# The first block of a convolution and MLP kernel: shift convolution in PSUM, a plan that knows of one shared port, carried spectra made last

## The chip, the cores and the metric

The kernel runs on one core of a Trainium2 chip. TensorE (PE in the profile) multiplies matrices into PSUM; VectorE (DVE) and ScalarE (ACT) work element by element on SBUF and PSUM; GpSimd (POOL) works on SBUF only; SyncE (SP) issues all DMAs of this kernel in one queue, in program order. The metric is the device time of one execution in microseconds, the median of the runs shown. Lower is better.

## The reference

Two kinds of layer alternate, twice: x = x + A(layernorm(x)), then x = x + B(layernorm(x)). x is 2048 tokens by 1024 channels, all in float32.

```python
def _A_ref(q, k, v, shift_k, ssm_k, ssm_D):
    k_shift = jnp.zeros_like(k)
    for t in range(ks):                       # ks = 4, causal, per channel
        k_shift = k_shift + k_pad[:, t:t + S, :] * shift_k[:, ks - 1 - t][None, None, :]
    kv = k_shift * v
    ...                                       # y = causal convolution of kv with ssm_k over all S, by FFT
    y = y + kv * ssm_D[None, None, :]
    return q * y                              # q = layernorm(x)
def _B_ref(x, w1, b1, w2, b2):
    h = jnp.einsum("bsd,df->bsf", x, w1) + b1
    h = relu(h) ** 2
    return jnp.einsum("bsf,fd->bsd", h, w2) + b2
```

k, v and the filter are the same in both A layers, so the long convolution's result y is computed once. F, the hidden width of B, is 3584.

## The kernel before

The 2048 tokens are four blocks of 512 (T). The long convolution is a blocked one: a block of 512 tokens is two halves of 256 (BL), each half is turned into a spectrum by matmuls with cosine and sine tables, spectra of inputs and of filter pieces are multiplied and added up, and matmuls turn them back. The complex product is done with three real ones: each spectrum is kept in three kinds (real part, imaginary part, and a sum or difference), and PAIRS says which kind of x meets which kind of the filter. The filter's spectra of a later block need a part of the block before, the "carried" spectrum, kept in DRAM as KD.

After the first block the kernel is one long list of steps: matmuls of the MLP on TensorE, each float32 product as three matmuls of a rounded part and a remainder (lines 327 to 329), and beside them the convolution's further blocks, spread over the steps by a pace (fwd_x, fwd_g, prod_stream). What this change touches most is the part before: first_block.

first_block has to do, before the MLP can start, for each of eight channel blocks c of 128 channels: load k, v and the filter; the shift convolution (line 1102 on ScalarE for the first tap, line 1105 three times on VectorE for the others, all in SBUF) and its product with v (line 1108, GpSimd or VectorE); TensorE's transposes (412) and forward matmuls for x (1076) and for the filter; the three kinds of each spectrum (ScalarE's 1124 and 1163, VectorE's 1126, 1165, 1167); the carried spectrum (TensorE, ScalarE's copy 1178, a store); the products per token half jj (1246, 1251, 1253), their combination (1257, 1258) and a butterfly (669, 670); the inverse matmuls; the gated output (1277), a copy of y for the second A layer (1280, stored as YD) and the residual add (1285). All these matmuls go through the helper fmm, so that they share line 1076. The D term enters as an addition to the filter's first row: line 1143, a VectorE add on one partition. LayerNorm's statistics (1187 and the small steps 1193 to 1207) are taken for two token tiles at a time at the start, and again at the end on the new x ("tail"), whose normalised rows TensorE transposes (1314); they are split into a rounded part and a remainder (1321, 1323). Four hidden tiles' weights (eight halves) are split as well (1333, 1334), and their matmuls on the first 256 tokens are the first MLP matmuls (327 to 329, 256 wide).

The order of all this is made by a planner, the class Plan. Each piece is a task with one or more possible engines and a cost on each, with the tiles it reads and writes. Tiles stand in rings of a few buffers, and a ring's buffers are given out in the order in which they were asked for. order() simulates the list: of the tasks that are ready it takes the one that can start earliest, and among these the one with the lowest priority value; rank is added to that value, so that the carried spectrum's matmuls (rank 2e6) come when nothing else is ready. 400 tries with varied priorities are made when the kernel is built, and the best is issued, engine by engine, in that order. The costs are the formulas v_cost, v2_cost (VectorE with two SBUF operands), g_cost and a_cost; DMAs are one engine "D" with 2 us of latency. Before, each engine was free of the others.

fill() issues transposes that nobody reads, to keep TensorE going; FILL has their numbers at three places: in the last inverse matmuls of the first block (38), in a later stage (45), and in the tail (17).

The buffers that matter here: sx and sg, the spectra (four channel blocks each); the banks p1 (two), p2 (four) and pt (two) in PSUM; and room within xh and xl, which hold the MLP's input later and in the first block k, the filter and the products.

Of the kernel before, what the change touches and what calls it, by code (L numbers as in the profile page):

```python
# [41 lines left out]
PLAN_TRIES = 400  # L42
NORM_0 = "VA"
# [6 lines left out]
FILL = (38, 45, 17)  # L50
# [45 lines left out]
class Plan:  # L96
# [37 lines left out]
    def order(self, rise, noise):  # L134
# [12 lines left out]
        while ready:  # L147
            best = None
            for i in ready:
# [20 lines left out]
            _, i, (e, c, st) = best  # L170
            _, _, _, bufs, lat, _ = self.tasks[i]
            free[e] = st + c
            end[i] = st + c + lat
# [13 lines left out]
    def run(self):  # L187
# [3 lines left out]
        for i in reversed(range(n)):  # L191
            opts, _, deps, _, lat, _ = self.tasks[i]
            self.height[i] += min(c for _, c in opts) + lat
            for d in deps:
                self.height[d] = max(self.height[d], self.height[i])
                self.after[d].append(i)
        rng = np.random.default_rng(1)
        best = None
        for k in range(PLAN_TRIES):
# [6 lines left out]
            got = self.order(rise, noise.tolist())  # L206
            if best is None or got[0] < best[0]:
                best = (*got, rise, noise)
# [13 lines left out]
def v2_cost(n):  # L222
    return 250 + 1.3 * n


def g_cost(n):
    return 200 + 2.45 * n
# [7 lines left out]
def tile_h3_mlp(ctx: ExitStack, tc: tile.TileContext, q, kT, vT, shk, ssmT, ssmD, w1, b1, w2, b2,  # L235
# [54 lines left out]
    V.memset(epst, EPS)  # L290

# [129 lines left out]
    def fwd_g(sb, c):  # L421
# [38 lines left out]
        V.tensor_add(oa[0], oa[1], k0)  # L460
# [50 lines left out]
    def prod_stream():  # L511
# [152 lines left out]
    def flat(t, e):  # L664
        return t[:, e].rearrange("p (n c) -> p n c", c=CG)

# [376 lines left out]
    def first_block():  # L1043
# [8 lines left out]
        def sub(tag, n, off, shape, nm="xh"):  # L1052
# [3 lines left out]
            def make():  # L1056
                v = big[nm].t[:, off + i * size:off + i * size + size]
                return v if len(shape) == 2 else v.rearrange("p (a b) -> p a b", a=shape[1])
# [8 lines left out]
        with tc.tile_pool(name="pro", bufs=1) as pro:  # L1067
# [31 lines left out]

            def x_part(c, k4, v4):  # L1100
                ks = new(cv, "fx", 4, [P, T])
                pl.add([("A", a_cost(T))], lambda e: A.activation(
                    ks.t, k4.t[:, 3:], AF.Copy, scale=shkt[:, c, 0:1]), [k4], [ks])
                for q_ in range(1, 4):
                    pl.add([("V", v2_cost(T))], lambda e, q_=q_: V.scalar_tensor_tensor(
                        ks.t, k4.t[:, 3 - q_:T + 3 - q_], shkt[:, c, q_:q_ + 1], ks.t,
                        op0=OP.mult, op1=OP.add), [k4], [ks], lat=130)
                pl.add([("G", g_cost(T)), ("V", v2_cost(T))], lambda e: ENG[e].tensor_mul(
                    ks.t, ks.t, v4.t), [v4], [ks])
# [5 lines left out]
                for r in range(2):  # L1115
# [8 lines left out]
                    pl.add([("A", a_cost(T))], lambda e, r=r, oi=oi: A.copy(spread(sp[r].t), sums(oi.t)), [oi], [sp[r]])  # L1124
                    if r:
                        pl.add([("V", v_cost(T))], lambda e, oi=oi: V.tensor_add(
                            spread(sp[2].t), sums(oi.t), spread(sp[0].t)), [oi, sp[0]], [sp[2]])
                for i in range(3):
                    dma(lambda i=i: dview(XD[i], 0, c), lambda i=i: sp[i].t, [sp[i]])

            def g_load(c):
                raw = sub("lg", 2, 1560, [P, T])
                aux = sub("la", 2, 2584, [P, P])
# [3 lines left out]
                dma(lambda: aux.t[0:1], lambda: bass.AP(tensor=ssmD.tensor, offset=ssmD.offset + c * P,  # L1137
                                                   ap=[[0, 1], [1, P]]), w=[aux], cost=10)
                return raw, aux

            def g_part(c, raw, aux):
# [8 lines left out]
                for r in range(2):  # L1150
# [11 lines left out]
                    if r == 0:  # L1162
                        pl.add([("A", a_cost(T))], lambda e, o=o: A.copy(spread(sp[0].t), sums(o.t)), [o], [sp[0]])
                    else:
                        pl.add([("V", v_cost(T))], lambda e, o=o: V.tensor_add(
                            spread(sp[2].t), sums(o.t), spread(sp[0].t)), [o, sp[0]], [sp[2]])
                        pl.add([("V", v_cost(T))], lambda e, o=o: V.tensor_sub(
                            spread(sp[1].t), sums(o.t), spread(sp[0].t)), [o, sp[0]], [sp[1]])
                o = bank("p1", 2, ps1)
                kd = new(cv, "fk", 2, [P, T])  # L1170

                def mmk(e):
                    for r in range(2):
                        for h in range(2):
                            s_ = slice(h * BL + P, h * BL + BL)
                            fmm(o.t[:, (2 * r + h) * P:(2 * r + h + 1) * P], base.t[:, 2 * h + r], raw.t[:, s_], True, True)
                pl.add([("PE", 900)], mmk, [*keys, *tabs], [o], rank=2e6)
                pl.add([("A", a_cost(T))], lambda e: A.copy(kd.t, o.t), [o], [kd])
                dma(lambda: KD[0][c], lambda: kd.t.rearrange("p (r n) -> p r n", r=2), [kd])
                for i in range(3):  # L1180
                    dma(lambda i=i: dview(GD[i], 0, c), lambda i=i: sp[i].t, [sp[i]])
# [8 lines left out]
            def moments(st, n):  # L1190
# [7 lines left out]
                pl.add([("V", 80)], lambda e: V.tensor_scalar(ve.t, mv.t[:, :, 1], EPS, None, op0=OP.add),  # L1198
                       al, [ve], lat=130)
                pl.add([("A", 190)], lambda e: A.activation(sd.t, mv.t[:, :, 1], AF.Sqrt, bias=epst), al, [sd])  # L1200
                pl.add([("V", 80)], lambda e: V.reciprocal(r.t, sd.t), [sd], [r], lat=130)
                pl.add([("V", 130)], lambda e: V.tensor_mul(t.t, r.t, r.t), [r], [t], lat=130)
                pl.add([("V", 130)], lambda e: V.tensor_mul(t.t, t.t, ve.t), [ve], [t], lat=130)
# [676 lines left out]
```

## Time and profile before

| what | value |
|---|---|
| median of three runs | 2758.64 us (2758.22 to 2763.38) |
| the profiled execution | 2754.0 us |
| its span, first to last instruction | 2752.2 us |
| mean granted TensorE clock | 0.995 |
| VectorE busy | 2010.1 us |
| GpSimd busy | 922.5 us |

A page of the profile describes one execution. "Busy" of an engine is the time in which one of its instructions was running, with whatever that instruction waited for once issued; the idle time before an instruction is given with the instruction that released it. A row of the table by window has, for each engine, busy us and the number of instructions, then the granted clock, the share of the DMA engines' time and the data rate. The time of the first block is the stretch from 0 to about 140 us.

### The profile page before, as it was taken

The page shows a single profiled execution, that of the slowest core. Times are in us where ns is not written, and L with a number is a line of the kernel's source. Part 1 is how long each engine was busy: PE and PEld are TensorE (multiplying, and loading weights), DVE is VectorE, ACT ScalarE, POOL GpSimd, SP SyncE. Part 2 cuts the span into 40 slices and gives each one's busy share as a digit, 9 for nine tenths or more (in the row PEclk, how much of TensorE's full clock was granted, in tenths as well). Part 3 has the DMA queues.
Part 4 walks back from the last instruction along what each step waited for, and adds up shares of the span by engine and source line. Part 5 has one row for each costly group of instructions (what it writes and reads, how often), then busy time and mean ns, then how long its engine had stood idle before and what let it go on. Part 6 is the DMA issues. An engine that isn't in the chain of part 4 may idle for free.

```text
span 2752.2 us, 36801 instructions
## 1 busy us (share of the span) xinstructions
PE 2696.8 (98%) x12632; PEld 2238.5 (81%) x12632; DVE 2010.1 (73%) x3109; ACT 1121.7 (41%) x1935; POOL 922.5 (34%) x655
## 2 busy tenths in 40 slices
PE   7899999899999999999999999999999999999999
PEld 6888787788888888888888888888788788878887
DVE  8879888779888877788777665366687666664555
ACT  4254344343444333342234422254455444445443
POOL 6926665155542655326544454000100010001000
PEclk9999999999999999999999999999999999999999
DMA  8489988689989898788987877688888866676546
GB/s 261 164 295 334 306 294 288 238 281 376 345 290 316 306 335 298 257 318 294 344 280 250 314 277 266 226 290 304 297 289 294 281 228 210 230 258 208 176 165 203
DMA packets 378876, 755.86 MB, mean 275 GB/s; under 512 B 43704, under 2 KB 160576, under 8 KB 378688
## 3 DMA queue, kind: packets, MB, share of 16 engines
q1 hardware_dynamic: 378688, 753.50, 79.7%
q8 instruction: 100, 1.64, 0.2%
q14 instruction: 88, 0.72, 0.1%
HBM read 603.41 MB, written 149.95 MB: 274 GB/s over the span
## 4 chain that ended last, share of the span: by engine, by line
PE 84%; DVE 6%; DMA 5%; POOL 2%; issue 1%; ACT 1%; SPq 1%; DVEq 0%; ACTq 0%; POOLq 0%
PE p L327 26%; PE p L329 26%; PE p L328 26%; DMA whl<-wd_m 1%; DMA wr<-w 1%; PE pt L329 1%; PE pt L328 1%; PE pt L327 1%; DVE whl L1005 1%; DMA cg<-gd 1%; DMA whl<-wd_t 1%; PE p L1076 1%; PE pt L446 0%; PE pt L412 0%; PE pt L588 0%
## 5 line engine op out<-in xcount | busy, mean ns | idle before, releaser
L517 POOL TENSOR_TENSOR cp<-cx,cg 128x384 f32<-128x384 f32 (+5 forms) x288 | 540.9, 1891 | 587.7 <-DVE sm L521 383.6
L327 PE MATMUL p<-xh,whl 128*128 128x512 f32 (+1 forms) x1840 | 707.7, 385 | 2.0 <-DMA whl<-wd_m 1.9
L329 PE MATMUL p<-xh,whl 128*128 128x512 f32 (+1 forms) x1840 | 703.8, 382 | 0.6 <-POOL whl L1005 0.6
L328 PE MATMUL p<-xl,whl 128*128 128x512 f32 (+1 forms) x1840 | 703.6, 382 | 0.3 <-DVE xl L1323 0.3
L997 ACT CAST whl<-wr 128x512 fp32r<-128x512 f32 x638 | 384.4, 618 | 458.1 <-PE p L329 269.6
L1005 DVE TENSOR_TENSOR whl<-wr,whl 128x512 fp32r<-128x512 f32 x624 | 506.1, 831 | 72.9 <-ACT whl L997 66.9
L327 PE MATMUL p<-whl,rh 128*128 128x512 f32 x1372 | 547.4, 399 | 6.1 <-DMA whl<-wd_m 4.5
L328 PE MATMUL p<-whl,rh 128*128 128x512 f32 x1372 | 542.4, 395 | 4.2 <-DVE whl L1005 4.2
L329 PE MATMUL p<-whl,rl 128*128 128x512 f32 x1372 | 541.8, 395 | 0.0
L327 PEld LDWEIGHTS p<-xh,whl 128*128 128x128 f32 x1840 | 346.4, 188 | 71.0 <-DMA whl<-wd_m 2.0
L329 PEld LDWEIGHTS p<-xh,whl 128*128 128x128 f32 x1840 | 346.2, 188 | 68.9 <-POOL whl L1005 0.8
L328 PEld LDWEIGHTS p<-xl,whl 128*128 128x128 f32 x1840 | 346.2, 188 | 66.4 <-DVE xl L1323 0.5
L327 PEld LDWEIGHTS p<-whl,rh 128*128 128x128 f32 x1372 | 258.8, 189 | 67.3 <-DMA whl<-wd_m 7.7
L328 PEld LDWEIGHTS p<-whl,rh 128*128 128x128 f32 x1372 | 258.9, 189 | 63.7 <-DVE whl L1005 6.4
L329 PEld LDWEIGHTS p<-whl,rl 128*128 128x128 f32 x1372 | 258.7, 189 | 60.3
L1504 POOL TENSOR_TENSOR acc<-acc,px 128x512 f32<-128x512 f32 x18 | 23.1, 1323 | 774.7 <-DMA px<-b 774.7
L1407 DVE TENSOR_TENSOR rl<-wr,rh 128x512 fp32r<-128x512 f32 x140 | 142.2, 1016 | 179.9 <-ACT rh L1402 179.8
L521 DVE TENSOR_REDUCE sm<-cp 128x128 f32<-128x384 f32 (+5 forms) x288 | 249.0, 873 | 7.9 <-POOL cp L517 7.9
L1399 ACT ACTIVATE wr<-p,b1t 128x512 f32<-128x512 f32 x138 | 95.2, 690 | 371.6 <-PE p L329 369.8
L1468 DVE TENSOR_TENSOR rl<-wr,rh 128x256 fp32r<-128x256 f32 x84 | 49.4, 588 | 206.4 <-ACT rh L1463 206.3
L1527 DVE TENSOR_TENSOR acc<-p,acc 128x512 f32<-128x512 f32 x152 | 101.2, 687 | 89.2 <-PE p L329 88.6
L1460 ACT ACTIVATE wr<-p,b1t 128x512 f32<-128x512 f32 x84 | 57.9, 689 | 187.5 <-PE p L329 187.5
(270 smaller groups left out, 3437.1 us busy)
## 6 DMA issues: line engine op xcount, KB each, us to landing
whl<-wd_m SPq DMA_DIRECT2D x382, 512.0 KB, 5.6
wr<-w SPq DMA_DIRECT2D x494, 256.0 KB, 5.2
wr<-td SPq DMA_DIRECT2D x152, 256.0 KB, 4.4
wd_m<-whl SPq DMA_DIRECT2D x70, 512.0 KB, 6.5
cx<-xd SPq DMA_DIRECT2D x48, 512.0 KB, 5.4
cg<-gd SPq DMA_DIRECT2D x48, 512.0 KB, 6.9
gd<-fg SPq DMA_DIRECT2D x72, 256.0 KB, 6.2
cx<-xd SPq DMA_DIRECT2D x48, 384.0 KB, 6.0
```

The lines of the kernel that those rows point to most:

```text
L327: PE.matmul(o, lh, rh, start=start, stop=False)
L328: PE.matmul(o, lh, rl, start=False, stop=False)
L329: PE.matmul(o, ll, rh, start=False, stop=stop)
L517: G.tensor_mul(pr.rearrange("p c i -> p i c"), xt[:, 0:j + 1], gt[:, j::-1])
L521: V.tensor_reduce(sm[:, ty, jj], st["pr"], axis=AX.X, op=OP.add)
L997: A.copy(t[:, 0], raws[n]["t"])
L1005: ENG[e[n % len(e)]].tensor_sub(t[:, 1], raws[n]["t"], t[:, 0].bitcast(F32))
L1399: A.activation(r, st["o"], AF.Relu, bias=b1t[:, st["f"]:st["f"] + 1])
L1407: V.tensor_sub(st["lo"], st["r"]["t"], st["hi"].bitcast(F32))
L1460: A.activation(r, st["o"], AF.Relu, bias=b1t[:, st["f"]:st["f"] + 1])
L1468: V.tensor_sub(st["lo"], r[:, 0:n], st["hi"].bitcast(F32))
L1527: V.tensor_add(accs[tt][:, d], o, accs[tt][:, d])
```

## The change

- The shift convolution's three VectorE steps read and write a PSUM bank (p2) in place of an SBUF tile; the product with v reads that bank and is VectorE's alone.
- The planner has one more resource, "port". Tasks marked with a third entry (VectorE's with two SBUF operands, the small LayerNorm steps, GpSimd's) hold their engine and the port. The costs are changed, and a factor lean makes VectorE look dearer when an engine is chosen.
- For seven of eight channel blocks the products of both token halves are made together (prods_both), in longer instructions: 6 in place of 17. For blocks 0 to 5 the inverse results of two channel blocks share a bank and are taken out together.
- The three kinds of a spectrum are one tile; the filter's third kind is made with the opposite sign, so that the two combinations become one add (fold). The later stages use the same sign and fold.
- The carried spectra are made after all other spectra, from two loads of their own (carry).
- The filter's first row plus D is made once for all blocks; each block gets its row by a small DMA.
- LayerNorm's first statistics are taken for all four tiles at once. ScalarE's table is loaded at the start (warm). The fillers are 16 and 8 in place of 38 and 17, the first of them in the last carried spectrum.

```diff
-FILL = (38, 45, 17)
+FILL = (16, 45, 8)
+PLAN_LEAN = (0, 0.5, 1)
...
-                for e, c in opts:
-                    st = max(t, free.get(e, 0.0))
-                    if f is None or st + c < f:
-                        f, pick = st + c, (e, c, st)
+                for e, c, *own in opts:
+                    st = max(t, free.get(e, 0.0), free.get("port", 0.0) if own else 0.0)
+                    late = st + c + lean * c * (e == "V")
+                    if f is None or late < f:
+                        f, pick = late, (e, c, st, own)
...
             free[e] = st + c
+            if own:
+                free["port"] = st + c
...
 def v2_cost(n):
-    return 250 + 1.3 * n
+    return 140 + 1.055 * n
 def g_cost(n):
-    return 200 + 2.45 * n
+    return 170 + 2.19 * n
...
+    warm = const.tile([P, 1], F32)
+    A.activation(warm, epst, AF.Copy)
...
-        V.tensor_add(oa[0], oa[1], k0)
+        V.scalar_tensor_tensor(oa[0], oa[1], -1.0, k0, op0=OP.mult, op1=OP.subtract)
...
-                E.tensor_add(s[:, 1], s[:, 0], s[:, 1])
-                E.tensor_sub(s[:, 2], s[:, 0], s[:, 2])
+                fold(E, s)
...
+    def fold(E, s):
+        E.tensor_add(s[:, 1:3], s[:, 1:3], s[:, 0:1].to_broadcast([P, 2, s.shape[2]]))
...
             def x_part(c, k4, v4):
+                kp = bank("p2", 4, ps2)
                 ks = new(cv, "fx", 4, [P, T])
                 pl.add([("A", a_cost(T))], lambda e: A.activation(
-                    ks.t, k4.t[:, 3:], AF.Copy, scale=shkt[:, c, 0:1]), [k4], [ks])
+                    kp.t, k4.t[:, 3:], AF.Copy, scale=shkt[:, c, 0:1]), [k4], [kp])
                 for q_ in range(1, 4):
-                    pl.add([("V", v2_cost(T))], lambda e, q_=q_: V.scalar_tensor_tensor(
-                        ks.t, k4.t[:, 3 - q_:T + 3 - q_], shkt[:, c, q_:q_ + 1], ks.t,
-                        op0=OP.mult, op1=OP.add), [k4], [ks], lat=130)
-                pl.add([("G", g_cost(T)), ("V", v2_cost(T))], lambda e: ENG[e].tensor_mul(
-                    ks.t, ks.t, v4.t), [v4], [ks])
+                    pl.add([("V", 750)], lambda e, q_=q_: V.scalar_tensor_tensor(
+                        kp.t, k4.t[:, 3 - q_:T + 3 - q_], shkt[:, c, q_:q_ + 1], kp.t,
+                        op0=OP.mult, op1=OP.add), [k4], [kp], lat=130)
+                pl.add([("V", v_cost(T))], lambda e: V.tensor_mul(ks.t, kp.t, v4.t), [v4, kp], [ks])
...
+            first = sub("la", 1, 2584, [P, 2 * P])
             def g_load(c):
...
+                dma(lambda: raw.t[0:1, 0:P], lambda: first.t[c:c + 1, 0:P], [first], [(raw, 0)], cost=10)
...
-                pl.add([("V", v_cost(P))], lambda e: V.tensor_add(raw.t[0:1, 0:P], raw.t[0:1, 0:P], aux.t[0:1]),
-                       [aux], [(raw, 0)])
...
+                        pl.add([("A", a_cost(T))], lambda e, o=o: A.activation(
+                            kind(sp, 2, GAT), sums(o.t), AF.Copy, scale=-1.0), [o], [(sp, GAT[2])])
...
+            def carry(half):
+                rows = new(pro, "s" + "xg"[half], 4, [P, 2, T])
+                dma(lambda: rows.t, lambda: ssmT[BL:T, half * T:half * T + T].rearrange("(m e) c -> m e c", e=2),
+                    w=[rows], cost=1460)
+                for c in range(4 * half, 4 * half + 4):
+                    carry_part(c, rows, slice(c % 4 * P, c % 4 * P + P))
+            def carry_part(c, rows, cols):
                 o = bank("p1", 2, ps1)
-                kd = new(cv, "fk", 2, [P, T])
+                kd = new(cv, "fg", 3, [P, T])
                 def mmk(e):
+                    if c == KT - 1:
+                        fill(o.t, FILL[0])
...
+                pl.add([("PE", 900)], mmk, [rows, *tabs[1:]], [o], rank=2e6)
                 pl.add([("A", a_cost(T))], lambda e: A.copy(kd.t, o.t), [o], [kd])
                 dma(lambda: KD[0][c], lambda: kd.t.rearrange("p (r n) -> p r n", r=2), [kd])
...
+            def prods_both(c):
+                xs, gs = spec["x", c], spec["g", c]
+                sm = sub("ppr", 2, 1024, [P, BT, 3, 2 * CU], "xl")
+                n = 3 * BL
...
+                rd = [(z, ty) for z in (xs, gs) for ty in range(3)]
+                pl.add([("G", g_cost(2 * n), 1), ("V", v2_cost(2 * n), 1)], lambda e: ENG[e].tensor_mul(
+                    slots(), both(xs), both(gs)[:, :, ::-1]), rd, [(sm, 0), (sm, 1)])
+                pl.add([("V", v2_cost(n), 1), ("G", g_cost(n), 1)], lambda e: ENG[e].tensor_add(
+                    at(1), at(0), at(1)), [(sm, 0)], [(sm, 1)])
+                pl.add([("G", g_cost(n), 1), ("V", v2_cost(n), 1)], lambda e: ENG[e].tensor_mul(
+                    at(0), both(xs)[:, :, 0], both(gs)[:, :, 0]), rd, [(sm, 0)])
+                pl.add([("G", g_cost(2 * T), 1), ("V", v2_cost(2 * T), 1)], lambda e: ENG[e].tensor_add(
+                    sm.t[:, :, 1:3], sm.t[:, :, 1:3], sm.t[:, :, 0:1].to_broadcast([P, BT, 2, 2 * CU])),
+                    [], [(sm, 0), (sm, 1)])
+                def turn(e):
+                    y = sm.t[:, :, 1:3].rearrange("p j r (n u c) -> p u j (r n) c", u=2, c=CG)
+                    f0 = sm.t[:, :, 0].rearrange("p j (n c) -> p j n c", c=CG)
+                    ENG[e].tensor_add(f0, y[:, 0], y[:, 1])
+                    ENG[e].tensor_sub(y[:, 0], y[:, 0], y[:, 1])
+                pl.add([("V", 2 * v2_cost(T), 1), ("G", 2 * g_cost(T), 1)], turn, [], [(sm, 0), (sm, 1)])
...
+                for jj in range(BT):
+                    behind(c, jj, sm, lambda jj=jj: z(jj), [(sm, jj)])
...
+            def behind(c, jj, sm, z, zk):
+                pair = c < KT - 2
+                h0 = BL * (c % 2) if pair else 0
+                o = bank("pt", 2, pst) if h0 == 0 else open_[jj]
...
-                g_part(c, *gl)
+                g_part(c, gl)
+                if c == KT - 1:
+                    carry(0)
+                    carry(1)
...
-                    for jj in range(BT):
-                        ln_part((2 * jj, 2 * jj + 1))
+                    ln_part(range(NT))
+                if c < KT - 1:
+                    prods_both(c)
                 for jj in range(BT):
-                    prods(c, jj)
+                    if c == KT - 1:
+                        prods(c, jj)
```

More of the change, by code (lines that the diff above doesn't have):

```diff
@@ L132, in add, with order @@
         return i
-    def order(self, rise, noise):
+    def order(self, rise, noise, lean):
         n = len(self.tasks)
@@ new lines, in g_part @@
+                for i in range(3):
+                    dma(lambda i=i: dview(GD[i], 0, c), lambda i=i: sp.t[:, GAT[i]], [(sp, GAT[i])])
+            def carry(half):
[4 more added lines that the diff above has]
+                    carry_part(c, rows, slice(c % 4 * P, c % 4 * P + P))
@@ L1264, in back @@
                 def back(e):
-                    if c == KT - 1 and jj == BT - 1:
-                        fill(o.t, FILL[0])
                     for h in range(2):
-                        oe = o.t[:, h * P:h * P + P]
+                        oe = o.t[:, h0 + h * P:h0 + h * P + P]
                         for r in range(2):
-                            fmm(oe, base.t[:, (5, 4, 3, 2)[2 * h + r]], z[h][:, r], r == 0, r == 1)
-                pl.add([("PE", 900)], back, [(sm, 0), (sm, 1), *tabs], [o])
@@ L1272, in prods @@
-                yo = new(cv, "fx", 4, [P, BL]) if c == KT - 1 else sub("yo", 2, 0, [P, BL], "xl")
-                yn = new(cv, "fk", 2, [P, 2, P])
-                sl = slice(c * P, (c + 1) * P)
+                            fmm(oe, base.t[:, (5, 4, 3, 2)[2 * h + r]], z()[h][:, r], r == 0, r == 1)
+                pl.add([("PE", 900)], back, [*zk, *tabs[1:]], [(o, h0)])
+                if pair and h0 == 0:
+                    return
+                w = 2 if pair else 1
+                cs = range(c + 1 - w, c + 1)
@@ L1275, in prods @@
+                ov = lambda: o.t[:, 0:w * BL].rearrange("p (w e c) -> p e w c", w=w, e=2)
+                oks = [(o, BL * i) for i in range(w)]
+                yo = new(cv, "fx", 4, [P, T]) if c == KT - 1 else sub("yo", 2, 0, [P, T], "xl")
+                yn = new(cv, "fk", 2, [P, 2, 2 * P])
+                sl = slice(cs[0] * P, (c + 1) * P)
+                as_w = lambda t: t.rearrange("p (w c) -> p w c", w=w)
                 for e_ in range(2):
                     tt = 2 * jj + e_
-                    pl.add([("V", v_cost(P))], lambda e, e_=e_, tt=tt: V.scalar_tensor_tensor(
-                        yn.t[:, e_], o.t[:, e_ * P:e_ * P + P], 1.0 / BL, ns[tt].t[:, sl],
-                        op0=OP.mult, op1=OP.mult), [o, (ns[tt], c // 4)], [(yn, e_)])
@@ L1350, in first_block @@
             for c in range(KT):
-                for kind in "xg":
-                    spec[kind, c] = [new(pro, "s" + kind, 12, [P, 2, BT, CU]) for _ in range(3)]
+                for k in "xg":
+                    spec[k, c] = new(pro, "s" + k, 4, [P, 3, 2, BT, CU])
+            dma(lambda: first.t[0:KT, 0:P], lambda: ssmT[0].rearrange("(c d) -> c d", d=P), w=[(first, 0)], cost=10)
+            dma(lambda: first.t[0:KT, P:], lambda: ssmD.rearrange("(c d) -> c d", d=P), w=[(first, 1)], cost=10)
+            pl.add([("V", v_cost(P))], lambda e: V.tensor_add(first.t[0:KT, 0:P], first.t[0:KT, 0:P], first.t[0:KT, P:]),
+                   [(first, 1)], [(first, 0), first])
             gl = g_load(0)
```

119 lines of the change are left out of this document (68 added, 51 removed).

## The prediction

> **What bounds the kernel now.** I read the page first, then a table by stage (busy time of each engine in chosen windows), then the order of time on TensorE.
>
> ```profile
> span 2752.2 us, 36801 instructions
> PE 2696.8 (98%) x12632; PEld 2238.5 (81%) x12632; DVE 2010.1 (73%) x3109; ACT 1121.7 (41%) x1935; POOL 922.5 (34%) x655
> ```
>
> TensorE is busy for 98% of the span: over the whole kernel nothing but its work counts, so a change of VectorE work can pay only where TensorE waits. The windows (TensorE, weight loads, VectorE, ScalarE, GpSimd, then granted clock, DMA share, GB/s) show where that is.
>
> ```profile
> 0.00:11.00 11.00, 0.00 (x0) 0.00 (x1) 4.31 (x7) 2.73 (x3) 2.41 (x7) 1.00 0.72 222
> 11.00:20.50 9.50, 9.50 (x46) 8.50 (x47) 7.06 (x14) 3.81 (x6) 0.00 (x0) 1.00 1.03 348
> 20.50:60.00 39.50, 35.63 (x206) 32.08 (x205) 38.78 (x68) 19.12 (x36) 33.79 (x34) 0.96 0.85 269
> 60.00:104.00 44.00, 40.36 (x243) 36.46 (x242) 40.91 (x64) 12.39 (x24) 42.23 (x44) 0.96 0.58 188
> 104.00:120.40 16.40, 14.97 (x84) 13.73 (x85) 14.53 (x25) 3.98 (x8) 15.90 (x17) 0.90 0.47 153
> 120.40:140.45 20.05, 15.26 (x105) 13.16 (x104) 15.99 (x41) 4.91 (x11) 12.92 (x17) 0.91 0.41 149
> 140.45:165.00 24.55, 24.21 (x199) 23.96 (x200) 10.44 (x22) 12.52 (x22) 6.14 (x5) 1.00 0.95 326
> 165.00:700.00 535.00, 517.51 (x2557) 435.46 (x2556) 447.82 (x653) 226.01 (x404) 282.56 (x219) 0.99 0.88 302
> ```
>
> The cuts are those of the first block. On TensorE:
>
> ```profile
> 11.00 1.13 PE L412 MATMUL p<-ident,fx 128*128 128x128 f32 x4 [11.00 <-POOL fx L1108]
> ...
> 120.43 1.06 PE L1076 MATMUL p<-xh,yh 128*128 128x128 f32 x8
> 122.28 1.52 PE L1076 MATMUL pt<-sm,yh 128*128 128x128 f32 x8 [0.80 <-POOL sm L669]
> 125.95 2.02 PE L1076 MATMUL pt<-sm,yh 128*128 128x128 f32 x8 [2.15 <-POOL sm L669]
> 127.77 5.36 PE L260 MATMUL pt<-ident 128*128 128x128 f32 x38
> 134.44 1.52 PE L1076 MATMUL pt<-sm,yh 128*128 128x128 f32 x8 [1.31 <-POOL sm L669]
> 136.00 1.08 PE L1314 MATMUL p<-ident,cp 128*128 128x128 f32 x8
> 136.92 2.02 PE L260 MATMUL p<-ident 128*128 128x128 f32 x17
> ...
> 140.45 0.39 PE L327 MATMUL p<-xh,whl 128*128 128x256 f32 x1
> ```
>
> It starts at 11.00, ends its forward transforms at 120.4 (the carried spectrum of the last channel block at 120.43 is the last of them), does filler transposes twice, and starts the MLP's matmuls at 140.45; the next window has it busy for 24.21 of 24.55. So **140.45 is the mark**: what moves it moves the end, if later stages keep their length.
>
> Between 11.00 and 140.45 TensorE loses, by window, 39.50 - 35.63 = 3.9, 3.6, 1.4 and 4.8 us idle, 13.7 in all. The granted clock takes 0.04, 0.04, 0.10 and 0.09 of these windows, 1.6 + 1.8 + 1.6 + 1.8 = 6.8 us. The fillers are 5.36 + 2.02 = 7.4 us. That leaves 129.45 - 13.7 - 6.8 - 7.4 = 101.5 us of useful work at full clock. Two gaps follow: in the middle (20.5 to 120.4) 8.9 idle + 5.0 clock = 13.9; in the endgame (120.4 to 140.45) 4.8 + 1.8 + 7.4 of filler = 14.0, beside 6.1 of work.
>
> Why it waits: VectorE and GpSimd both read as busy in the middle, yet GpSimd's column and VectorE's hide waits for each other. First GpSimd, then VectorE, in the same stretch:
>
> ```profile
> 35.68 1.50 POOL L1334 TENSOR_TENSOR whl<-wr,whl 128x512 fp32r<-128x512 f32 x1
> 37.13 0.92 POOL L1246 TENSOR_TENSOR sm<-sx,sg 128x256 f32<-128x256 f32 x1
> ```
> ```profile
> 36.08 1.37 DVE L670 TENSOR_TENSOR sm<-sm 128x256 f32<-128x256 f32 x1
> 37.38 0.68 DVE L1167 TENSOR_TENSOR sg<-p,sg 128x512 f32<-128x512 f32 x1
> 37.98 0.14 DVE L1203 TENSOR_TENSOR rt<-rt,ve 128x2 f32<-128x2 f32 x1
> ```
>
> VectorE's L670 is issued at 36.08 and ends only after GpSimd's L1334 has; then GpSimd's L1246 takes 0.92 instead of its shortest 0.72 (below). L1167, with one operand in PSUM, is not touched by GpSimd beside it. So two-operand SBUF work of the two engines goes one at a time; I call that the port. Start to start, L1167 takes 0.60.
>
> ```profile
> L1105 DVE SCALAR_TENSOR_TENSOR fx<-xh,shkt,fx x24: 732/752/1830, 6.4 to 101.9; 128x512 f32<-128x512 f32 x24
> L1251 POOL TENSOR_TENSOR xl<-sx,sg x14: 1262/1294/1712, 20.8 to 113.7; 128x512 f32<-128x512 f32 x14
> L1251 DVE TENSOR_TENSOR xl<-sx,sg x7: 673/1012/1753, 59.1 to 114.1; 128x512 f32<-128x512 f32 x7
> L1246 POOL TENSOR_TENSOR sm<-sx,sg x14: 723/754/2042, 24.3 to 123.0; 128x256 f32<-128x256 f32 x14
> L1246 DVE TENSOR_TENSOR sm<-sx,sg x10: 409/533/1522, 21.5 to 123.1; 128x256 f32<-128x256 f32 x10
> L1165 DVE TENSOR_TENSOR sg<-p,sg x8: 673/674/678, 24.0 to 122.0; 128x512 f32<-128x512 f32 x8
> L457 DVE SCALAR_TENSOR_TENSOR pt<-fk,sgn,pt x24: 741/747/751, 172.6 to 1411.0; 128x512 f32<-128x512 f32 x24
> ```
> ```profile
> L1187 DVE BATCH_NORM_STATS2 st<-cg 128x6 f32<-128x512 f32 x8 | 5.4, 682 | 0.3 <-POOL cg L1285 0.3
> ```
>
> The columns are shortest/median/longest, in the last row busy time and mean. From the shortest at 256 and 512 elements: VectorE 0.145 + 1.03 ns per element (0.08 less at the head of a row of instructions, by L1167's start to start), GpSimd 0.18 + 2.1 ns. Work put on GpSimd therefore holds the port about 2.05 times as long.
>
> **The change, part by part.** *Shift convolution in PSUM.* L1105's 24 instructions and the product L1108 after them leave the port. No instruction of the first block has the new form, but L457 has it exactly: SBUF, scalar, PSUM into PSUM, 747 ns and never above 751, against 732 at best and 1830 at worst for L1105. I take 0.67 in a row, the bounds being 0.65 and 0.75. The product, SBUF times PSUM, is priced by L1165.
>
> [...]
>
> *Products in longer instructions.* Per channel block (128 channels, eight of them) the products still touch 5120 elements a lane, in 6 instructions instead of 17 for seven of the eight: at VectorE's price 6 x 0.08 + 5.12 x 1.03 = 5.75 us instead of 6.6.
>
> *One port in the plan.* It costs nothing by itself. What it can reach I work out as a balance, for the work up to the last forward transform, at VectorE's price. Free of the port, per channel: 3 x 0.67 + 0.60 + 3 x 0.60 (L1126, L1165, L1167), and 0.7 for the gated output, 5.1. On the port: 5.75, the residual add 0.7, one weight split 0.6, 7.05. Seven channels give 85; LayerNorm's statistics (12 x 0.60, L1187 in a row), its halves and small steps add about 11, of which 3.7 on the port; the outputs taken two blocks at once and the small steps for four tiles at once are in these sums. So VectorE would have 96, with 53 of them on the port. Moving a to GpSimd makes 96 - a = 53 + 1.05a, a = 21, and both at **75 us**; GpSimd then holds the port for 43.
>
> What TensorE leaves for it: 101.5 less the 6.1 of the endgame and less the carried spectra, eight times about 0.9 (1.06 in the row at 120.43, with the overlap taken off), 7.2: 88.2. From VectorE's first convolution at 6.4 to 11 + 88.2 = 99 are 93 us, so each of the two would be in use for 81%. TensorE becomes the bound, and the middle's gap should shrink but not go: 0 to 13.9, I take half, 7.
>
> *Carried spectra last.* Their 7.2 us of matmuls leave the middle and fill the endgame, where there were 7.4 us of filler; the fillers go from 55 to 24, about 3.2 us by the rows. Eight ScalarE copies and eight stores move with them and two loads of 512 KB are added, on SP's queue behind the last spectra; the stores are first read by the next block's conv stream, after the mark.
>
> ```profile
> x<-cx SPq DMA_DIRECT2D x2, 512.0 KB, 2.6
> yd<-xl SPq DMA_DIRECT2D x14, 128.0 KB, 2.0
> xh<-pro SPq DMA_DIRECT2D x1, 512.0 KB, 5.3
> ```
>
> A load of that size lands in 2.6 to 5.3 us. It needs a spectrum slot, which is free only once an older block's products are done; behind it on TensorE's bank ring stand the tail's transposes. The chain to them took from 120.4 to 136.0, 15.6 us, so 5.3 + 7.2 is covered by about 3 us; without that cover it costs its lateness. In the endgame before, the results of the last block but one were waited for until 125.95, 5.5 us. With the port at 81% most of that goes; the endgame then lasts between its work, 6.1 + 7.2 = 13.3, and the old 20.05. I take 16.
>
> *First row by DMA.* One VectorE add on one partition per block goes; a small DMA with a wait for the load takes its place, landing about 2 us later by the smallest row above. Behind it on SP stand the next block's loads, one block ahead: 0, or 2 us where the prefetch is short.
>
> *Start.*
>
> ```profile
> 4.34 1.28 ACT L1102 ACT_TABLE_LOAD   x1 [4.34 <-DMA xh<-kT]
> 4.85 0.47 SPq L1065 DMA_DIRECT2D xh<-pro  x1
> 9.24 1.71 POOL L1108 TENSOR_TENSOR fx<-fx 128x512 f32<-128x512 f32 x1 [7.93 <-DVE fx L1105]
> ```
>
> The table load goes ahead of the data (1.28), the product goes from GpSimd's 1.71 to 0.68; but the tables for the matmuls (issued 4.85, 5.3 to land) come at about 10. I take 1 us of a possible 2. The sign moved into the spectra adds a ScalarE copy per block; ScalarE is at 12.39 of 44. The edits of the main stage (one fold instead of two instructions, one other VectorE form) lie under TensorE's matmuls: 0.
>
> The granted clock is 0.91 in the endgame in spite of 55 fillers. [...]
>
> **Sum.** 10 + 88.2 + 7 + 16 = 121.2 for the mark instead of 140.45, 19.2 us earlier. The profiled execution took 2754.0 (span 2752.2); it would become 2734.8. The three runs lie at 2758.22 to 2763.38, median 2758.64, 4.6 above the profiled one; carried over, the forecast is **2739.4**. Its bounds: 9 + 88.2 + 0 + 13.3 = 110.5, 30 us earlier, 2728.7; and 11 + 88.2 + 13.9 + 20 = 133.1, 7.3 earlier, 2751.3.
>
> **Rivals.** *VectorE and the port stay the bound:* the middle keeps its 13.9, the endgame 19: mark at 131, 9.4 earlier, 2749.2. For it: 81% on two engines that lock each other is much for a schedule fixed beforehand. Against: 3 x 0.65 + 0.60 = 2.6 us per block leave the port.
>
> *The gap only moves:* the carried spectra were what TensorE did in the middle while it waited, and the products are now one chain of long links. Middle 13.9 + 7.2, endgame 20: 139.3, 2757.5, no change. For it: TensorE waits for sm in the rows above; against: the port's load falls.
>
> *Long holds, slower:* a product of 1536 elements on GpSimd holds the port 0.18 + 2.1 x 1.536 = 3.4 us. If VectorE always comes to a port instruction at once, every hold is VectorE's wait. The last transform is then at 6.4 + 75 + 43 = 124.4, and with the endgame of 20 the mark is 144.4, 2762.6, still within the bound below; if the plan gives GpSimd 30 instead of 21 (62 us of hold, 66 for VectorE) it is 154.4, 2772.6, slower. It decides from 39 of the 43 us on. Against: of the 75 us that VectorE keeps, 7 x 5.1 + 7.2 = 43 are free of the port, and L1105's median was 752 while GpSimd was busy for 42.23 of 44.
>
> *Given back later:* an earlier start changes what the conv stream meets in the window 165 to 700, where TensorE idles 535 - 517.51 = 17.5. Half of that again, 9: 2748.
>
> **How the numbers follow.** Forecast 0.57, VectorE's bound 0.20, given back 0.04, gap moves 0.10, long holds 0.09. The first three are faster by more than 0.2% (5.5 us, about what a measurement of this kernel can tell from no change): 0.81; same 0.10; slower 0.09. The range takes the first three and the bounds: 2729 to 2752, 0.81.
>
> **What would show it.** Right: TensorE's first 256-wide MLP matmul near 121 and its waits for sm in the middle halved; the convolution at 0.75 throughout; VectorE's shortest and mean product times close. Wrong: the same idle in the middle with both engines busy (the bound stays); TensorE waiting on the carried rows' load; VectorE's port instructions of 3 us and more (long holds); a mark near 121 with an unchanged end (given back).

## The result and the profile after

The changed kernel takes 2742.56 us (median of 6 runs, 2739.37 to 2745.52), the kernel before 2758.27 beside it (6 runs, 2755.12 to 2763.38). The ratio is 0.9943, with a 95% interval of 0.9932 to 0.9953: 15.7 us, 0.6%, faster. The profiled execution took 2739.37, with this page:

```profile
span 2737.6 us, 36599 instructions
PE 2689.7 (98%) x12601; PEld 2233.3 (82%) x12601; DVE 1992.1 (73%) x3068; ACT 1125.0 (41%) x1937; POOL 844.5 (31%) x531
```

TensorE is still busy for 98%. The span is 14.6 us shorter. The table by window, cut at the same events as before (busy us and instructions of TensorE, its weight loads, VectorE, ScalarE, GpSimd; then granted clock, DMA share, GB/s):

```profile
0.00:9.50 9.50, 0.00 (x1) 0.03 (x1) 3.24 (x6) 2.18 (x3) 0.70 (x6) 1.00 0.61 182
9.50:20.50 11.00, 10.06 (x40) 8.41 (x41) 5.49 (x10) 2.88 (x6) 0.00 (x0) 1.00 0.93 266
20.50:101.40 80.90, 78.89 (x468) 71.90 (x467) 76.39 (x108) 34.48 (x60) 38.59 (x28) 0.98 0.78 251
101.40:123.51 22.11, 17.36 (x146) 15.95 (x144) 19.43 (x51) 10.78 (x21) 6.94 (x8) 1.00 0.81 291
...
148.00:683.00 535.00, 511.82 (x2516) 429.82 (x2515) 446.13 (x648) 223.23 (x399) 272.55 (x196) 0.99 0.88 297
```

The middle, from 20.5 to the end of the last forward transform, is 80.9 us long, where it was 99.9. TensorE idles there for 80.90 - 78.89 = 2.0 us and loses 0.02 x 80.9 = 1.6 to its clock: a gap of 3.6, where it was 13.9. GpSimd, which was busy for 91.93 us of the old middle, now is for less than half of it. The endgame, from there to the mark, is 22.11 us long, where it was 20.05. TensorE in order of time, around the endgame:

```profile
9.50 1.10 PE L419 MATMUL p<-ident,fx 128*128 128x128 f32 x4 [9.50 <-DVE fx L1128]
11.54 2.90 PE L1089 MATMUL p<-fg,yh 128*128 128x256 f32 x6 [0.94 <-DMA yh<-fwd]
...
100.82 0.59 PE L1089 MATMUL p<-fg,xh 128*128 128x256 f32 x2
101.25 1.05 PE L1089 MATMUL pt<-xl,yh 128*128 128x128 f32 x8
104.05 2.02 PE L1089 MATMUL p<-sx,yh 128*128 128x128 f32 x16 [1.75 <-DMA sx<-ssmT]
105.91 1.95 PE L1089 MATMUL pt<-xl,yh 128*128 128x128 f32 x16
...
113.25 1.16 PE L1089 MATMUL p<-sg,yh 128*128 128x128 f32 x8 [0.92 <-ACT fg L1212]
114.24 1.91 PE L265 MATMUL p<-ident 128*128 128x128 f32 x16
...
117.67 1.13 PE L1089 MATMUL pt<-sm,yh 128*128 128x128 f32 x8 [0.63 <-DVE sm L678]
119.42 1.36 PE L1393 MATMUL p<-ident,cp 128*128 128x128 f32 x8 [0.62 <-ACT cp L1253]
120.62 1.04 PE L265 MATMUL p<-ident 128*128 128x128 f32 x8
121.91 0.66 PE L1393 MATMUL p<-ident,cp 128*128 128x128 f32 x4 [0.25 <-DVE xl L1402]
123.10 0.66 PE L1393 MATMUL p<-ident,cp 128*128 128x128 f32 x4 [0.53 <-DVE xl L1402]
123.51 0.36 PE L334 MATMUL p<-xh,whl 128*128 128x256 f32 x1
```

The mark, the first 256-wide MLP matmul, is at 123.51: 16.9 us earlier than 140.45. The carried spectra are the matmuls with sx and sg at the left of yh; the first of them waits 1.75 us for its load. L265 are the fillers. Between the mark and the end 2.3 us are given back.

What the shift convolution costs now, and its product (shortest/median/longest):

```profile
L1125 DVE SCALAR_TENSOR_TENSOR p<-xh,shkt,p x24: 740/756/758, 5.8 to 92.2; 128x512 f32<-128x512 f32 x24
L1128 DVE TENSOR_TENSOR fx<-p,fx x8: 681/691/692, 8.7 to 93.0; 128x512 f32<-128x512 f32 x8
```

Nothing stretches them any more: the longest is 758 ns, where it was 1830.

### The profile page after: what moved, and what is told of

Same layout as the page of the kernel before. It is cut to its first block, busy times and chain, and to the rows that moved or that the text cites. A ratio compares the mean times of both kernels' runs of the same rounds, so it can differ in the third digit from the quotient of the medians.

```text
span 2737.6 us, 36599 instructions
## 1 busy us (share of the span) xinstructions
PE 2689.7 (98%) x12601; PEld 2233.3 (82%) x12601; DVE 1992.1 (73%) x3068; ACT 1125.0 (41%) x1937; POOL 844.5 (31%) x531
## 4 chain that ended last, share of the span: by engine, by line
PE 85%; DMA 7%; DVE 5%; issue 1%; POOL 1%; ACT 1%; SPq 1%; DVEq 0%; ACTq 0%; POOLq 0%
PE p L334 26%; PE p L335 26%; PE p L336 26%; PE p L1089 2%; DMA whl<-wd_m 1%; DMA wr<-w 1%; DMA cg<-gd 1%; PE pt L335 1%; PE pt L336 1%; PE pt L334 1%; DVE whl L1014 1%; DMA wd_m<-whl 1%; DMA whl<-wd_t 1%; DMA cx<-xd 1%; POOL cp L524 0%
```

## The experiments

**The question.** The total came out near the forecast, but the change is a bundle. Theory: the port's load was the bound, so that what takes work off the port, the convolution in PSUM, carries the gain, and the carried spectra pay because TensorE has no gaps left in the middle. Rivals: the plan that knows of the port does it; the longer products do it; or the order that the planner happened to find does. Each experiment is read by its mark (one profiled execution each), by the gap of the middle worked out as above (the clock has two digits, so a gap is good to about 0.5 us), and by its time against the kernel before. The mark and the time do not always move alike, so both are given.

| run | mark, us | middle: length, gap, us | endgame, us | time to before, 95% interval |
|---|---|---|---|---|
| before | 140.45 | 99.9, 13.9 | 20.1 | 1 |
| the change | 123.51 | 80.9, 3.6 | 22.1 | 0.9943 (0.9932 to 0.9953) |
| e1_conv_sbuf | 135.69 | 91.3, 13.5 | 23.9 | 0.9971 (0.9960 to 0.9982) |
| e2_no_port | 126.6 | 83.9, 5.2 | 22.2 | 0.9942 (0.9927 to 0.9957) |
| e3_carry_mid | 132.13 | 91.3, 8.5 | 20.3 | 0.9958 (0.9942 to 0.9975) |
| e10_carry_mid16 | 132.33 | 90.3, 6.2 | 21.5 | 0.9959 (0.9944 to 0.9974) |
| e4_split | 127.33 | 84.4, 4.8 | 22.4 | 0.9949 (0.9935 to 0.9964) |
| e5_seed2 | 127.06 | 85.1, 6.3 | 21.5 | 0.9956 (0.9941 to 0.9971) |
| b1_psum_only | 130.72 | 90.9, 5.0 | 19.3 | 0.9963 (0.9951 to 0.9975) |
| b2_port_only | 142.55 | 94.9, 9.7 | 27.2 | 0.9999 (0.9989 to 1.0009) |
| b3_psum_port | 134.48 | 93.8, 7.3 | 20.2 | 0.9973 (0.9964 to 0.9982) |
| b4_psum_carry | 137.80 | 94.5, 17.5 | 22.8 | 0.9962 (0.9947 to 0.9976) |
| e8_last_g | 122.05 | 81.2, 3.7 | 20.4 | 0.9919 (0.9903 to 0.9936) |
| e6_tries | 121.57 | 79.5, 2.4 | 21.6 | 0.9922 (0.9907 to 0.9936) |

### e1_conv_sbuf: the change without its PSUM convolution

```diff
-                kp = bank("p2", 4, ps2)
...
-                    pl.add([("V", 750)], lambda e, q_=q_: V.scalar_tensor_tensor(
-                        kp.t, ..., kp.t, ...), [k4], [kp], lat=130)
-                pl.add([("V", v_cost(T))], lambda e: V.tensor_mul(ks.t, kp.t, v4.t), [v4, kp], [ks])
+                    pl.add([("V", 750, 1)], lambda e, q_=q_: V.scalar_tensor_tensor(
+                        ks.t, ..., ks.t, ...), [k4], [ks], lat=130)
+                pl.add([("G", g_cost(T), 1), ("V", v2_cost(T), 1)], lambda e: ENG[e].tensor_mul(ks.t, ks.t, v4.t), [v4], [ks])
```

> The changed kernel with the shift convolution and its product back in SBUF (and the plan told that they hold the port). The mark is the start of the first 256-wide MLP matmul: 140.45 before, 123.51 after. Theory (the port bounds the first block): 3 x 0.66 + 0.60 = 2.6 us per channel block go back on the port, the balance of VectorE and port rises from 75 to about 84 us of 92, and the mark comes 5 to 10 us later, 129 to 133. Rival (VectorE's own load bounds it, whatever the port): VectorE has the same instructions as long as before, so the mark stays within 2 us of 123.5.

The mark is at 135.69, 12.2 later: past the theory's own range, and far from the rival's. Its two windows, the product on GpSimd, and two of TensorE's waits in the middle (us in total, times, longest):

```profile
20.50:111.80 91.30, 83.28 (x475) 74.94 (x474) 79.76 (x111) 36.42 (x63) 28.37 (x19) 0.94 0.73 229
111.80:135.69 23.89, 18.75 (x137) 17.93 (x136) 20.04 (x53) 10.23 (x20) 4.03 (x6) 0.86 0.65 236
```
```profile
L1127 POOL TENSOR_TENSOR fx<-fx x6: 1269/2084/2735, 14.1 to 102.8; 128x512 f32<-128x512 f32 x6
```
```profile
PE p L1089 <- ACT fg L1132: 4.3, 2, 3.6
PE p L419 <- POOL fx L1127: 1.6, 2, 1.2
```

The middle's gap is back: 8.0 idle + 0.06 x 91.3 = 13.5, where it was 13.9 before the change. The plan put six of the eight products on GpSimd, and there they take 2084 ns in the median, against 1269 at their shortest: now it is GpSimd that waits for the port, ahead of TensorE's transposes. Not all of the gap is the port's, though. TensorE waits only 1.6 us for these products directly. The longest single wait, 3.6 us, is for a ScalarE copy of transposed data (L1132) that stood behind ScalarE's normalisation steps, which looks like a matter of this run's order. So 12.2 overstates what the convolution's place costs; in the time it is 0.0028, 7.7 us, with intervals that do not meet.

### b1_psum_only: the PSUM convolution alone, in the kernel before

The edit is the reverse of e1's, in the kernel before, whose plan knows no port.

> The kernel before with one part of the change alone: the shift convolution and its product through PSUM. Theory (the port's load bounds the first block): 2.6 us per channel block leave the port, 21 us in all, though the plan still does not know of the port; mark 6 to 12 us before the old 140.45, 128 to 134. Rival (without a plan that knows the port nothing is gained): mark within 2 us of 140.45.

```profile
20.50:111.40 90.90, 87.76 (x539) 80.21 (x538) 84.22 (x158) 37.81 (x70) 83.16 (x97) 0.98 0.76 238
111.40:130.72 19.32, 14.64 (x104) 13.19 (x102) 13.75 (x37) 5.02 (x11) 11.80 (x15) 0.91 0.51 179
```

The mark is at 130.72, 9.7 earlier; the middle's gap falls from 13.9 to 3.1 + 1.8 = 5.0, while GpSimd stays busy for 83.16 of 90.90. So this one part takes some 9 us of TensorE's waiting away, and its removal in e1 brings 10 back: the theory's first half is shown from both sides, in the time as well (0.0037, 10.2 us, by itself). It needs no plan that knows of the port. The edit does two things at once: the three convolution steps leave the port, and their product, which GpSimd made for three of the eight channel blocks, becomes VectorE's. They were not tried apart; b2 below bears on it.

### e2_no_port and b2_port_only: the plan's part, taken out and alone

```diff
                 for e, c, *own in opts:
+                    own = []
...
-PLAN_LEAN = (0, 0.5, 1)
+PLAN_LEAN = (0,)
...
-    return 140 + 1.055 * n
+    return 250 + 1.3 * n
...
-    return 170 + 2.19 * n
+    return 200 + 2.45 * n
```

> The changed kernel with the planner's port, lean and new cost formulas taken out; all other parts stay. Theory (the port must be known to the plan): the plan gives GpSimd more, its holds stretch VectorE's port instructions as before, TensorE's gap in the middle returns: mark 5 to 10 us later, 129 to 134. Rival (the lighter port load alone does it): mark within 2 us of 123.5.

The mark is 3.1 later, between the two, and the time is that of the change. The first 100 us of the change and of this run:

```profile
0.00:100.00 100.00, 87.55 (x499) 79.10 (x500) 83.73 (x121) 39.23 (x67) 37.89 (x33) 0.98 0.78 246
```
```profile
0.00:100.00 100.00, 85.39 (x481) 76.87 (x482) 76.99 (x109) 39.58 (x67) 42.92 (x36) 0.98 0.75 242
```

GpSimd is busy for 42.92 instead of 37.89: without the port the plan splits the work nearly the same way, so there was little for the port to correct. The middle's gap, 5.2, did not return to 13.9 as the theory had it. b2 gives the kernel before the port, lean and costs, with the tasks marked as in the change:

> The kernel before with the plan's part of the change alone: port, lean and the new costs, with the same tasks. By the balance with the convolution on the port, VectorE and port need 91 of the 93 us. Theory (load, not order): at 98% no order helps much, mark 136 to 141. Rival (the order is what counts): mark 8 us or more earlier, below 132.

The mark is at 142.55 and the time unchanged: just past the range of the theory, which was that no order helps at this load. GpSimd went from 74.44 us busy in the first 100 to 33.79, so VectorE took its work; the middle became shorter (94.9) and the endgame longer (27.2). The rival, below 132, is out. The convolution and its product in b2:

```profile
L1110 DVE SCALAR_TENSOR_TENSOR fx<-xh,shkt,fx x24: 732/744/753, 6.7 to 100.6; 128x512 f32<-128x512 f32 x24
L1113 DVE TENSOR_TENSOR fx<-fx x7: 672/678/685, 9.1 to 101.4; 128x512 f32<-128x512 f32 x7
```

Here, with all of it in SBUF, the plan alone keeps the convolution from being stretched (753 ns at most) and puts seven of the eight products on VectorE, and the mark does not come earlier. So neither the product's engine nor the end of the stretching is enough by itself; what b1 has besides is the load taken off the port.

### b3_psum_port: both

> The kernel before with the convolution in PSUM and the plan with the port; products per half, carried spectra per block and first row as before. Theory (parts add): the mark of the run with PSUM alone, less what the plan alone gave, 126 to 133; what is left to 123.5 is the longer products and the carried spectra. Rival (the plan gives nothing beside PSUM): within 2 us of the run with PSUM alone.

134.48 is neither: above the theory's 133 and 3.8 above b1's 130.72. With the plan added, PSUM alone became no faster: the plan shows no gain there, and 3.8 is about what another order makes, as the next run shows.

### e5_seed2: how much is luck

```diff
-        rng = np.random.default_rng(1)
+        rng = np.random.default_rng(2)
```

> The changed kernel with another seed of the planner's random tries: the same work in another order of equal standing. It measures how far luck of the plan moves the mark: all theories expect 121 to 126 and a time within 3 us of the changed kernel. A move of 5 us or more would mean that the single removals are not told from luck.

The mark is at 127.06, 3.6 later and just outside what all theories expected, and the run is 0.0013 of the time, 3.6 us, slower than the change. A single seed is one draw, but it sets a scale: moves of 3 to 4 us of the mark are not told from the planner's luck. That covers e2 (3.1), e4 (3.8) and the step from b1 to b3 (3.8); it does not cover e1 (12.2), b1 (9.7), nor e3 and e10 below (8.6 and 8.8). A third order of the same work, e6 at the end with a longer search, has its mark at 121.57, so that the three lie up to 5.5 us apart.

### e4_split: shorter products

> The changed kernel with the products of every channel block made per token half, in 15 instructions instead of 6, as the changed kernel does it for the last block alone. Theory (fixed costs per instruction on the port count): 9 more instructions for each of 7 blocks, 0.08 us each on VectorE to 0.18 on GpSimd, 5 to 11 us more load at 81% use: mark 2 to 6 us later, 125.5 to 129.5. Rival (shorter holds interleave better): mark the same or earlier, 121 to 124.

The products of all eight blocks are made by prods(c, jj). The mark is at 127.33, within the theory's range, but 3.8 later is about what luck makes. That the longer instructions help is likely by the shortest times in the kernel before (products of 256 and 512 elements: VectorE 409 and 673 ns, GpSimd 723 and 1262, so half the length costs more than half the time); these runs do not show it in the mark.

### e3_carry_mid and e10_carry_mid16: carried spectra per block

```diff
-            def carry_part(c, rows, cols):
+            def carry_part(c, raw, keys):
...
-                pl.add([("PE", 900)], mmk, [rows, *tabs[1:]], [o], rank=2e6)
+                pl.add([("PE", 900)], mmk, [*keys, *tabs[1:]], [o], rank=2e6)
...
                 g_part(c, gl)
-                if c == KT - 1:
-                    carry(0)
-                    carry(1)
```

> The changed kernel with the carried spectra made per channel block again, from the block's own filter tile, and fillers 38 and 17 as before. Theory (TensorE is the bound in the middle, VectorE in the endgame): 7.2 us of TensorE work go into a middle without gaps, the last transform ends about 7 us later, the endgame stays about 21 us long: mark 5 to 8 us later, 129 to 131. Rival (the carried spectra were free fillers in either place): mark within 2 us of 123.5.

The mark is at 132.13, 8.6 later and 1.1 past the theory's range. But its 38 fillers ran to where the next result was ready, so they might have been the cause; e10 has 16 and 8.

> The run with the carried spectra per block again (its mark 132.1), but with the change's fillers, 16 and 8, in place of 38 and 17. Theory (the place of the carried spectra counts): mark still 128 to 131, 4 us or more over the change's 123.5 and beyond the 3.6 that another seed gave. Rival (the long fillers did it: after them TensorE found the next result already there): mark 123 to 127, no more than luck of the plan.

132.33, again past the theory's range, by 1.3, and far from the rival's: the place counts, not the fillers. In the time, e3 and e10 are 4.1 and 4.4 us slower than the change, about half of what the mark moved, and their intervals overlap the change's.

```profile
20.50:110.80 90.30, 85.93 (x524) 78.69 (x523) 79.94 (x117) 39.56 (x69) 40.25 (x28) 0.98 0.75 241
110.80:132.33 21.53, 13.97 (x81) 13.14 (x79) 16.41 (x43) 6.16 (x13) 5.32 (x6) 0.76 0.51 180
```

TensorE in order of time, the two longest waits of that endgame:

```profile
117.54 1.94 PE L1089 MATMUL pt<-sm,yh 128*128 128x128 f32 x8 [4.04 <-DVE sm L678]
...
125.54 2.05 PE L1089 MATMUL pt<-sm,yh 128*128 128x128 f32 x8 [3.47 <-DVE sm L678]
```

The middle is 9.4 us longer: 6.8 more of matmuls at full clock (85.93 - 1.8 against 78.89 - 1.6; seven of the eight carried spectra are in it) and 2.6 more of gap. The endgame, with little in it for TensorE to do meanwhile (13.97 busy of 21.53), is only 0.6 shorter; some of its length is the slow clock after those two waits (0.76).

### b4_psum_carry: would the two parts do?

The kernel before with PSUM and with the carried spectra last (rows in four of its smaller spectrum slots, fillers 16 and 8).

> The kernel before with two parts of the change: the convolution in PSUM, and the carried spectra last with fillers 16 and 8. Plan, costs, products, first row and the rest as before. Theory (these two make the gain): mark 123 to 127, from 130.7 with PSUM alone. Rival (the longer products and the plan are needed for the endgame): mark 129 to 132.

Both were wrong: 137.80, 7.1 later than with PSUM alone.

```profile
20.50:115.00 94.50, 85.46 (x476) 75.83 (x475) 86.53 (x156) 30.64 (x58) 79.73 (x96) 0.91 0.65 208
115.00:137.80 22.80, 18.56 (x137) 17.04 (x136) 19.30 (x42) 9.55 (x19) 13.99 (x17) 0.93 0.74 261
```
```profile
37.78 0.68 DVE L1109 TENSOR_TENSOR fx<-p,fx 128x512 f32<-128x512 f32 x1
38.61 1.10 PE L412 MATMUL p<-ident,fx 128*128 128x128 f32 x4 [4.45 <-DVE rs L1213]
```

The middle has some 9 us less of matmuls at full clock (85.46 - 8.5 against 87.76 - 1.8) and lasts 3.6 longer than b1's: its gap is 9.0 + 8.5 = 17.5, against 5.0. The reading that fits is that the carried work had been what TensorE did while it waited for VectorE and GpSimd (busy for 86.53 and 79.73 of 94.50); taken out, it left a hole. The longest wait, 4.45 us, is put down by the profile to a small LayerNorm step (L1213), but the transpose reads fx, and the product that makes it (L1109) ended at 38.46, just before: it is VectorE's convolution that came late. No second seed of this variant was run, so the size is open. And the time does not show the loss at all: 0.9962, where b1 has 0.9963, each good to about 4 us.

### e8_last_g and e6_tries: what is left

e8 gives the products of the last channel block's second half to GpSimd alone, which in the change stood still for 9 us of the endgame. One of its four edited tasks:

```diff
-                    pl.add([("G", g_cost(T), 1), ("V", v2_cost(T), 1)], lambda e, ty=ty, pr=pr: ...
+                    pl.add([("G", g_cost(T), 1)] if jj else [("G", g_cost(T), 1), ("V", v2_cost(T), 1)], lambda e, ty=ty, pr=pr: ...
```

> The changed kernel with the products of the last block's second token half on GpSimd alone. In the endgame VectorE was busy for 18.77 of 21.31 us and did about 3 us of these products while GpSimd stood still. Theory (VectorE's queue sets the length of the endgame): mark 1 to 4 us earlier, 119.5 to 122.5. Rival (the chain from the last load and its latencies sets it, or GpSimd's holds take it back): mark 123 or later.

GpSimd's long rest in the change, and the two windows of e8:

```profile
120.74 0.45 POOL L1363 TENSOR_TENSOR cg<-cg,fk 128x128 f32<-128x128 f32 x1 [8.99 <-DVE fk L1354]
```
```profile
20.50:101.70 81.20, 77.47 (x466) 70.29 (x464) 75.74 (x115) 36.28 (x62) 44.09 (x28) 1.00 0.81 257
101.70:122.05 20.35, 16.18 (x138) 15.33 (x137) 15.17 (x36) 10.75 (x20) 10.76 (x13) 1.00 0.71 247
```

The mark is at 122.05, within the theory's range. But VectorE's work in the endgame fell by 4.3 us (19.43 to 15.17) and the endgame by 1.8, and the mark by less than the scale of luck. So VectorE's queue is at most a part of what sets it.

> The changed kernel with 3000 tries of the planner in place of 400: the same work in a better order by the plan's own measure. Theory (the order is within luck of its best): mark 121 to 125. Rival (the plan's order leaves much): mark below 120.

PLAN_TRIES is 3000 here, and the mark is at 121.57, as the theory had it. Both runs are faster than the kernel before by 0.8% (0.9919 and 0.9922). They were not timed beside the change, their intervals touch that of the change (up to 0.9936 against 0.9932 at the least), and their marks, 1.5 and 1.9 earlier, explain only a part of the 6 us. So these are the versions to prefer, with a difference to the change that is probable, not shown.

## Why the prediction was right, and where it was not

**The bound** was read rightly. TensorE waited in the first block for work that VectorE and GpSimd could only do one at a time, and the mark moved the end: 16.9 us at the mark, 14.6 in the span, 15.7 in the medians, against 19.2 forecast (2739.4 forecast, 2742.56 measured).

**The convolution in PSUM** costs what L457 promised: 756 ns in the median against 747. Over the same steps in SBUF that is little: the medians differ by 4 (756 against L1105's 752), the shortest by 8 (740 against 732), and b2's convolution in SBUF, which nothing stretched, has a median 12 lower (744).

**The middle** was forecast with half its gap, 7; it kept 3.6, nearly all of it one wait of 1.85 us before 39.04 and the slow clock behind it (0.50 from 40 to 42 us). With the start, taken as 10 and measured at 9.5, the last transform ended at 101.4 instead of 105.2. TensorE's waits for sm are gone from it. That TensorE would become the bound there was right; the balance behind it was not what came. Up to 101.4 VectorE was busy for 3.24 + 5.49 + 76.39 = 85.1 us instead of 75, which is 89% of the time from its first convolution at 5.8, not 81%; GpSimd, at 39.3, was near the forecast 43. How much of VectorE's 10 us more was waiting for the port and how much was work missing from the sum stays open. Even so it held TensorE up but little.

**The endgame** is the step that failed: forecast 16, between bounds of 13.3 and 20.05; it took 22.1, outside them. The 16 was 13.3 of work and 2.7 for everything else. That is less than the fillers alone, which the prediction itself kept at about 3.2, so it left no room for any wait. (The 13.3 also has one carried spectrum twice, 0.9: the one at 120.43 lies in the old endgame's 6.1 already.) By the rows above, the 22.1 were 2.95 of fillers, 22.11 - 17.36 = 4.75 idle, and 14.4 of other matmuls. The wait that the prediction did name is gone: the results of the last channel block but one are used at 105.91 without one. What it put at nothing came in its place: 1.75 for the carried rows' load, which the forecast had covered by 3 us, 0.92 for a ScalarE copy, and 2.0 in four waits for the last block's results. In no run was the endgame under 19.3, with VectorE busy for 13.75 (b1) or 20.04 (e1): with the carried spectra in it 20.4 to 23.9, without them 19.3 to 21.5, and 27.2 in b2. I read it as the length of a chain, from the last spectrum over products, inverse, output, statistics and normalisation to the split, on four engines in turn; no run tests that, and what one could take from it beyond e8's 1.8 us was not tried.

**The plan with one port** was priced at nothing by itself, with a balance that it could reach. It shows no gain in either direction beyond luck. The mark came out 2.3 us off because two errors were opposite, 3.8 too late for the middle and 6.1 too early for the endgame; that closeness is luck. Another 2.3 were given back after the mark: in the window of 535 us behind the block TensorE's idle time went from 17.49 to 23.18, 5.7 more, of which later stages made up a part. That was a rival, at 9 us. It is one profile against one, and what makes it was not tried.

**The rivals.** *VectorE and the port stay the bound* forecast a mark at 131: e1, at 135.69 with the middle's old gap, is near what it looks like, and it needs the convolution on the port. *The gap only moves* is what b4 did. *Long holds* did not happen: the plan put all seven of the 1536-element products on VectorE (x7 below), and GpSimd had one instruction over 2 us in the first block, of 2.36.

```profile
L1284 DVE TENSOR_TENSOR xl<-sx,sg 128x1536 f32<-128x1536 f32 x7 | 12.7, 1813 | 0.7 <-PE pt L1089 0.6
```

**The clock.** The change's endgame has 24 fillers, the carried spectra, no wait over 1.75 us, and a granted clock of 1.00. e10, without the carried spectra there, has the two waits of 4.04 and 3.47 us and a granted clock of 0.76 over 21.5 us, 5.2 us' worth: the eight matmuls after the one took 1.94 us and those after the other 2.05, where the eight before the first wait took 1.06. How long a wait brings this on, the runs do not tell: in b3 it follows one of 2.07 us (the rows below, the eight matmuls before that wait and the eight after it), while e8 keeps 1.00 over its endgame with a wait of 2.67.

```profile
115.15 1.06 PE L1081 MATMUL pt<-sm,yh 128*128 128x128 f32 x8
118.28 2.04 PE L1081 MATMUL pt<-sm,yh 128*128 128x128 f32 x8 [2.07 <-DVE sm L674]
```

## What to carry to other kernels

When VectorE and GpSimd both read as busy and their instructions are longer than their shortest, look for what they share: moving one operand to PSUM took the convolution out of GpSimd's way for 4 to 12 ns an instruction, and brought 9.7 of the mark's 16.9 us by itself. Moving filler work to the end moved the mark forward by 8.8 us where the engines that feed TensorE had room (e10 to the change: GpSimd busy for 40.25 of 90.30), and back by 7.1 where both were busy nearly throughout (b1 to b4: 84.22 and 83.16 of 90.90). TensorE's own gap in the middle does not tell the two cases apart (6.2 and 5.0), and each is one run against one. And where a search makes the order, change its seed before crediting a part with 3 us, and do not take an early milestone for the time: b4's mark is 7.1 later than b1's, and their times agree within their intervals.

## What the runs showed of the hardware that was not expected

As far as these rows show, the port is held for a whole instruction, and the wait falls on whichever engine comes second. In the kernel before it was VectorE's convolution that was stretched (longest 1830 ns); in e1, with few GpSimd instructions, the convolution had a median of 746 (longest 1746) and GpSimd's product one of 2084, against 1269 at its shortest. One of these products, started 0.3 us after a VectorE product of 1.75 us:

```profile
52.25 1.75 DVE L1284 TENSOR_TENSOR xl<-sx,sg 128x1536 f32<-128x1536 f32 x1
52.57 2.57 POOL L1127 TENSOR_TENSOR fx<-fx 128x512 f32<-128x512 f32 x1 [6.07 <-PE p L1089]
```

It ends at 55.14, 1.14 us after VectorE's does at 54.00, which is near its own shortest time of 1.27. And a GpSimd that is busy for 83 of 91 us (b1) still left TensorE with a gap of 5.0 in the middle: being busy nearly all the time, with the port, did not by itself hold up the rest once VectorE's chain in front of the transposes was off it.
